# Block-sparse attention before a long-convolution block on one Trainium2 core: mask rows of three head pairs issued from ScalarE's DMA queue, and the last result copied in halves

## The chip, the core and the metric

The kernel runs on one core of one Trainium2 chip. The metric is the device time of the whole program in microseconds (us); lower is better. TensorE (PE in the profile) multiplies matrices, VectorE (DVE), ScalarE (ACT) and GpSimd (POOL) do the rest, SyncE (SP) only issues transfers here. Each engine works through its own instructions in their order, and a semaphore wait holds up all that stands behind it on that engine.

## What is computed

```python
# attention: q, k, v are (4, 8, 768, 64), blocks of 64 positions
k_rep = k.reshape(B, H, 12, 64, D).mean(axis=3)
gate = einsum('bhsd,bhnd->bhsn', q, k_rep)      # future blocks: -1e9
sel = top 3 blocks of gate for each row, and the row's own block
scores = where(sel & causal, q @ k.T / 8, -1e9)
x = softmax(scores) @ v                          # to (4, 768, 512)
# long convolution and gates
x1, x2, x3 = split(x @ w_proj, 3)                # w_proj (512, 1536)
conv = irfft(rfft(x2, axis=1) * rfft(filter_fft, axis=0), axis=1)
out = (x1 * conv * x3) @ w_out                   # float32 (4, 768, 512)
```

## The kernel before

The 32 heads are handled as 16 pairs (p = 0 to 15, four to a batch element). Each head of a pair takes three slots, so a pair has six and the program 96. In a slot n, PE makes the scores of slot n+1 (`scores`, L562, into one of two PSUM buffers, tag "sc", L138), ACT takes the exponential of slot n (L571), POOL zeroes the upper triangles (L574), and PE multiplies the exponentials of slot n-1 with the values (`products`, L596). After a head's third slot DVE divides by the sums (L604, L605) and frees the one PSUM accumulator of the products.

The selected blocks enter the scores as extra contraction rows. For head 0 of pair p the moving operand is `TQ[p % 3]` (its tile is named TQL): rows 0 to 63 hold q transposed, and rows 64 to 75 one mask row for each block. For head 1 it is `QB[p % 2]`, built alike. The stationary operands `KA[p % 2]` and `KB[p % 3]` hold k transposed and twelve rows that mark the blocks. What is made for a pair ahead of its slots:

- q: loaded by SP (`load`, L153), turned by PE (L387) and copied by ACT with all 128 rows into TQ (`copy_q`, L459), with a rest by DVE (L464). From pair five on, ACT casts q (`cast_q`, L471), DVE splits it (L476) and a transposing DMA turns it (L482). Then `part_q` (L485, SP) sends rows 64 to 127 of TQ, the second head's q, to QB.
- k: loaded and turned alike, cast by ACT into KH (`cast_k`, L404), block sums by DVE (L407), and sent by `send_k` (L413 to KA, L414 to KB, both SP).
- mask: PE makes the gate (L490, L496), DVE takes the eight largest of each row and compares (L505, L508, L511), PE turns the result (`turn_mask`, L521), and ACT copies it into `M16[p % 2]` (`copy_mask`, L532). Pairs 0 and 1 write TQ and QB directly; from pair 2 on `send_mask` (L540 to TQ, L541 to QB) sends the rows by DMA, 12 rows of 768 halves each. As these land on rows that `part_q` reads, L540 waits for that pair's L485.

In the first batch element the spectrum of the filter is made beside the attention: SP loads it (`load_filter`, L314, L315), PE reverses it (L332), DVE folds it (L333, L334), PE transforms it (L349), and ACT and DVE turn it by twiddle factors (L370, L376). From pair 4 on the convolution of the batch element before runs in the same slots (`hyena`); the last one runs in a tail after the last slot. There `output` multiplies by w_out (L734), copies the PSUM result (L737) and SP sends it (L738). The last of the tail is O5.

The order is written out by hand in the table ORDER. A time is in sevenths of a slot; `placed` (L816) takes "name.p" if there is one and else adds 42 p to "name:" with p modulo 4. `at` puts the piece into its slot, and the main loop (L889) emits the pieces place by place.

```python
def placed(name, p):
    n0 = 2 * NS * p
    own = ORDER.get(f"{name}.{p}")
    return own if own is not None else 7 * n0 + ORDER[f"{name}:{p % DC}"]
```

In the built program the transfers of SP and ACT share eight semaphores, which are handed out in turn; a transfer waits until the one that had its semaphore before has landed.

Of the kernel before, what the change touches and what calls it, by code (L numbers as in the profile page):

```python
# [37 lines left out]
    "td:3": -48, "kr:3": -57, "g:3": -43, "m:3": -43, "mt:3": -32, "mc:3": -29, "md:3": -28,  # L38
    "v:3": -4, "x:3": 55, "f:3": 66, "k0.1": 1, "k1.1": 1, "q0.1": 11, "q1.1": 13, "kc0.1": 2,
    "ks0.1": 3, "qc0.1": 11, "qr0.1": 13, "kc1.1": 7, "ks1.1": 1, "qc1.1": 13, "qr1.1": 14,  # L40
    "kd.1": 13, "qd.1": 17, "kr.1": 13, "g.1": 18, "m.1": 19, "mt.1": 31, "mc.1": 31, "md.1": 84,
    "k0.2": 12, "k1.2": 27, "q0.2": 31, "q1.2": 39, "kc0.2": 28, "ks0.2": 19, "qc0.2": 37,
    "qr0.2": 39, "kc1.2": 30, "ks1.2": 29, "qc1.2": 39, "qr1.2": 45, "kd.2": 34, "qd.2": 42,
    "kr.2": 42, "g.2": 49, "m.2": 50, "mt.2": 59, "mc.2": 59, "md.2": 62, "k0.3": 51, "k1.3": 61,
    "q0.3": 67, "q1.3": 75, "kc0.3": 55, "ks0.3": 63, "qc0.3": 71, "qr0.3": 79, "kc1.3": 67,
    "ks1.3": 63, "qc1.3": 77, "qr1.3": 80, "kd.3": 67, "qd.3": 92, "kr.3": 66, "g.3": 83, "m.3": 87,
    "mt.3": 100, "mc.3": 102, "md.3": 109, "v.1": 13, "v.2": 53, "v.3": 112, "ldv.2": 23,
    "ldk.3": 11, "ldq.3": 40, "ldv.3": 83, "x.0": 65, "x.1": 105, "x.2": 151, "MN": 6, "flip": 4,
    "cos": 10, "wo": 233, "rows0": 5, "rows1": 28, "rows2": 59, "M0": 43, "M1": 42, "lf0": 18,
    "IC0": 44, "IS0": 32, "ff0": 80, "s00": 109, "s10": 123, "tA00": 128, "tA10": 144, "tB00": 132,  # L50
    "tB10": 136, "t200": 148, "t210": 157, "lf1": 18, "IC1": 42, "IS1": 58, "ff1": 95, "s01": 137,
    "s11": 143, "tA01": 162, "tA11": 168, "tB01": 163, "tB11": 176, "lf2": 81, "IC2": 35, "IS2": 70,
    "ff2": 102, "s02": 158, "s12": 157, "tA02": 175, "tA12": 186, "tB02": 180, "tB12": 196,
# [2 lines left out]
    "hc:0": -94, "hl:0": -100, "hd:0": -85, "hs:0": -66, "hc:1": -86, "hl:1": -75, "hd:1": -64,  # L56
    "hs:1": -57, "hc:2": -117, "hl:2": -114, "hd:2": -99, "hs:2": -110, "hc:3": -94, "hl:3": -93,
    "hd:3": -76, "hs:3": -74, "mq:0": -31, "mq:1": -29, "mq:2": -30, "mq:3": -27, "mq.1": 31,
    "mq.2": 75, "mq.3": 102, "direct": 2,
    "open": ["id32", "zeros", "lq0", "halves", "angles", "lk0", "lk1", "lv0", "twists", "sp0",  # L60
        "sp1", "own", "sp2", "sr0", "w14", "w2", "biasl", "lq1", "MN0", "period", "sr2", "sr1",
        "biasr", "q0", "sm0", "qc0", "q1", "id16", "sm2", "qc1", "qd", "qr0", "sm1", "w8",
        "qr1", "k0", "k1", "ks0", "se2", "ks1", "kc0", "kc1", "se1", "se0", "w2", "kr", "kd",
        "st1", "st2", "st0", "g", "table", "w13", "lk2", "lv1", "m", "rows", "w1", "mt", "ones",
        "ma", "lq2", "mb", "v", "s", "sel16", "late"],
    "mid": [("P00", 29), ("P11", 35), ("P02", 38), ("P01", 44), ("P12", 48), ("F00", 63),
        ("P10", 67), ("X01", 70), ("F10", 74), ("X02", 74), ("F01", 75), ("X00", 83), ("F11",
        92), ("F02", 94), ("F12", 103), ("X03", 103), ("X11", 112), ("X10", 116), ("I3", 122),
# [23 lines left out]
def kernel(  # L92
# [10 lines left out]
    nc = tc.nc  # L103

    B, H, S, D = q.shape
    P = 128
    SC = S // P
    NB = S // 64
    Dm = H * D
# [31 lines left out]
    def one(name, shape=(P, 512), dtype=FP32):  # L141
        return ps.tile(list(shape), dtype, name=name, tag="one", bufs=3)
# [109 lines left out]
    MN = [const.tile([P, SC, P], fp, name=f"MN{i}") for i in range(2)]  # L252
    V16 = [const.tile([P, SC, 2, 66], fp, name=f"V16_{i}") for i in range(3)]
    KA = [const.tile([P, S], fp, name=f"KA{i}") for i in range(2)]
    KB = [const.tile([P, S], fp, name=f"KB{i}") for i in range(3)]

    TQL = [const.tile([P, 2 * SC - 1, P], fp, name=f"TQL{i}") for i in range(3)]
    TQ = [t[:, 0:SC, :].rearrange("p c s -> p (c s)") for t in TQL]
    QL = [t[:, SC - 1:2 * SC - 1, :].rearrange("p c s -> p (c s)") for t in TQL]
    QB = [const.tile([P, S], fp, name=f"QB{i}") for i in range(2)]  # L260
# [40 lines left out]
    flip = const.tile([P, P], FP32, name="flip")  # L301
# [3 lines left out]
    wo = const.tile([P, DC, Dm], fp, name="wo")  # L305
# [104 lines left out]

    def send_k(p):
        kh = KH[p % 2]
        nc.sync.dma_start(KA[p % 2][0:D, :], kh[0:D, :])  # L413
        nc.sync.dma_start(KB[p % 3][0:D, :], kh[D:P, :])  # L414


    def cast_k16(p):
# [96 lines left out]
    M16 = [const.tile([P, S], fp, name=f"M16_{i}") for i in range(2)]  # L514
# [22 lines left out]
                                scalar2=None, op0=ALU.mult)  # L537

    def send_mask(p):
        nc.sync.dma_start(TQ[p % 3][64:64 + NB, :], M16[p % 2][64:64 + NB, :])  # L540
        nc.sync.dma_start(QB[p % 2][64:64 + NB, :], M16[p % 2][96:96 + NB, :])  # L541

# [92 lines left out]
    def hyena(b, spread):  # L637
# [3 lines left out]
        def other(step):  # L641
            return ("m" if spread else "t") + step in ORDER["swap"]
# [20 lines left out]
        def single(step, name, small_bank):  # L663
            return one(name) if small_bank != other(step) else sc_tile()[:, 0:512]
# [66 lines left out]
        def output(i):  # L731
            op = one("op") if spread else single(f"O{i}", "op", True)
            for cc in range(DC):
                nc.tensor.matmul(op, lhsT=st["yT"][:, cc, P * i:P * (i + 1)], rhs=wo[:, cc, :],  # L734
                                 start=(cc == 0), stop=(cc == DC - 1))
            osb = outp.tile([P, Dm], FP32, name="osb", tag="osb")
            (nc.vector.tensor_copy if other(f"C{i}") else nc.scalar.copy)(osb, op)  # L737
            late.append(lambda: nc.sync.dma_start(out[b, P * i:P * (i + 1), :], osb))  # L738

# [9 lines left out]
        for i in range(SC):  # L749
            steps[f"O{i}"] = lambda i=i: output(i)  # L750
# [16 lines left out]
    def ones_of_values():  # L767
# [7 lines left out]
        "biasl": bias_left, "biasr": bias_right, "own": own_blocks,  # L775
        "MN0": lambda: nc.vector.memset(MN[0], 0.0), "rows": mask_rows, "late": constants_late,
        "ones": ones_of_values, "qd": lambda: part_q(0), "kd": lambda: send_k(0),
        "table": lambda: nc.scalar.preload_act_table_set("natural_log_exp_and_others"),
        "kr": lambda: prep_kr(0), "g": lambda: prep_gate(0), "m": lambda: prep_mask(0),
# [30 lines left out]
    def at(time, f):  # L810
        n, place = divmod(time, 7)
        assert n >= 0
        if n < slots:
            work[n][place].append(f)
# [7 lines left out]
    for p in range(NP):  # L822
# [5 lines left out]
        if p:  # L828
            if p < ORDER["kturned"]:
                for t in range(2):  # L830
                    ev += [(f"k{t}", lambda p=p, t=t: turn_k(p, t)),
                           (f"kc{t}", lambda p=p, t=t: cast_k(p, t)),
                           (f"ks{t}", lambda p=p, t=t: sum_k(p, t))]
            else:
                ev += [("hc", lambda p=p: cast_k16(p)), ("hl", lambda p=p: split_k(p)),
                       ("hd", lambda p=p: send_kh(p)), ("hs", lambda p=p: sum_k16(p))]
            ev += [("kd", lambda p=p: send_k(p))]
            if p < TURNED:
                for t in range(2):
                    ev += [(f"q{t}", lambda p=p, t=t: turn_q(p, t)), (f"qc{t}", lambda p=p, t=t: copy_q(p, t)),  # L840
                           (f"qr{t}", lambda p=p, t=t: rest_q(p, t))]
                ev += [("qd", lambda p=p: part_q(p))]
            else:
                ev += [("tc", lambda p=p: cast_q(p)), ("tr", lambda p=p: split_q(p)),
                       ("ts", lambda p=p: send_q(p)), ("td", lambda p=p: part_q(p))]
            ev += [("kr", lambda p=p: prep_kr(p)), ("g", lambda p=p: prep_gate(p)),
                   ("m", lambda p=p: prep_mask(p)), ("mt", lambda p=p: turn_mask(p)),
                   ("mc", lambda p=p: copy_mask(p)), ("v", lambda p=p: prep_v(p))]
            if p >= DIRECT:
                ev += [("md", lambda p=p: send_mask(p))]  # L850
            else:
                ev += [("mq", lambda p=p: copy_second_mask(p))]
# [29 lines left out]
            at(ORDER[name], f)  # L882
    for b in range(1, B):
        steps = hyena(b - 1, True)
        for name, time in ORDER["last" if b == B - 1 else "mid"]:
            at(7 * per * b + time, steps.pop(name))
        rest = steps

# [17 lines left out]
    tail = hyena(B - 1, False)  # L906
# [37 lines left out]
```

## Time and profile before

| | us |
|---|---|
| median of 3 runs | 252.03 |
| lowest and highest | 251.15, 253.54 |
| the profiled execution | 251.01 |
| its span | 249.3 |
| PE busy | 231.0 |
| DVE busy | 190.6 |
| ACT busy | 166.4 |
| POOL busy | 132.2 |

The span runs from the first to the last instruction of the profiled execution. A row of the timeline gives start, length, engine, line, operation, output and input tiles with shapes, and in brackets how long the engine stood idle before and what released it. "SPq" is SP's queue; a row of it is the issue, not the transfer's way to its landing. A row of the chain of work that ended last gives start, length and what it was. In a group's row "x27 | 12.9, 478" is the count, the busy time in us and the mean of one in ns.

### The profile page before, as it was taken

Reading aid. Unit: us, or ns where it says so; the run is one execution under the profiler, and the core shown is the slowest. Engines: PE = TensorE matmul, PEld = TensorE weight load, DVE = VectorE, ACT = ScalarE, POOL = GpSimd, SP = SyncE. Lnnn points to the kernel's source line nnn. Section 1 sums busy time; section 2 is a strip of 40 time slices with the busy share of each in tenths; the row PEclk is TensorE's granted clock in tenths of the full one; section 3 lists DMA queues with packets and bytes.
Section 4 is the critical chain, followed back from the end, with each engine's and each line's share of the span. In section 5 each row is a group of like instructions: output and inputs, shape, how many; then the busy total and the mean of one; then the engine's idle time right before and its main releaser. Section 6 shows DMA issues by size and latency. Waiting matters only on the chain.

```text
span 249.3 us, 6285 instructions
## 1 busy us (share of the span) xinstructions
PE 231.0 (93%) x2270; PEld 151.0 (61%) x2270; DVE 190.6 (76%) x558; ACT 166.4 (67%) x258; POOL 132.2 (53%) x248
## 2 busy tenths in 40 slices
PE   5888988899699999999999999999999999999993
PEld 4666865577556676666574666666656665544551
DVE  3676767878866998988568988896789777668981
ACT  4747975668798568696986577869856776422352
POOL 7623532635573568874432698754257586005560
PEclk9979999999999999999999999999999999999999
DMA  8998968999999996999999979979973111500015
GB/s 161 201 225 218 246 137 221 214 162 216 177 216 208 173 191 144 193 173 203 273 214 203 194 157 180 168 166 260 213 138 66 37 28 51 213 1 0 0 41 214
DMA packets 110295, 40.47 MB, mean 162 GB/s; under 512 B 100932, under 2 KB 106424, under 8 KB 110264
## 3 DMA queue, kind: packets, MB, share of 16 engines
q1 hardware_dynamic: 108008, 37.97, 76.4%
q0 software_dynamic: 2256, 2.10, 5.7%
q8 instruction: 18, 0.29, 0.5%
q14 instruction: 13, 0.11, 0.2%
HBM read 24.64 MB, written 6.29 MB: 124 GB/s over the span
## 4 chain that ended last, share of the span: by engine, by line
PE 70%; DMA 10%; DVE 7%; SPq 5%; ACT 4%; issue 2%; POOL 0%; ACTq 0%; DVEq 0%; POOLq 0%
PE sps L562 11%; PE op L734 7%; PE x2p L658 7%; PE x3p L722 6%; PE o L596 6%; PE x1p L719 6%; PE xx L671 4%; SPq L153 4%; DMA TQL<-M 3%; PE kt L387 3%; PE ye L699 3%; PE yo L702 3%; DMA q_nat<-in_q_dram 2%; DMA QB<-TQL 2%; DMA fb<-in_moe_filter_fft_dram 2%
## 5 line engine op out<-in xcount | busy, mean ns | idle before, releaser
L571 ACT ACTIVATE ex<-sps 128x896 f16<-128x896 f32 x96 | 87.6, 923 | 5.1 <-PE sps L562 4.8
L574 POOL TENSOR_SCALAR_AFFINE_SELECT ex<-ex 128x256 f16<-128x256 f16 x96 | 41.7, 437 | 77.6 <-ACT ex L571 74.0
L596 PEld LDWEIGHTS <-ex 128*128 128x128 f16 x672 | 32.9, 97 | 9.7 <-DVE xnat L605 1.0
L596 PE MATMUL o<-V,ex 128*128 128x65 f16 x672 | 36.4, 193 | 0.5 <-DVE xnat L605 0.2
L562 PE MATMUL sps<-TQL,KA 76*128 76x512 f16 (+1 forms) x144 | 26.4, 293 | 2.5 <-DMA TQL<-M 1.4
L691 POOL TENSOR_TENSOR yT<-gg,yy 128x384 f16<-128x384 f32 x23 | 22.9, 1015 | 8.0 <-DVE yy L708 3.5
L562 PE MATMUL sps<-QB,KB 76*128 76x512 f16 (+1 forms) x144 | 26.2, 290 | 0.2
L725 ACT CAST x1sb<-x1p 128x384 f16<-128x384 f32 x27 | 12.9, 478 | 19.2 <-PE x1p L719 19.1
L682 POOL TENSOR_TENSOR PQ<-ta 128x512 f16<-128x512 f32 x12 | 15.2, 1270 | 19.0 <-DVE ta L681 18.8
L658 PE MATMUL x2p<-wp,xf 128*128 128x512 f16 x96 | 24.2, 379 | 0.0
L719 PE MATMUL x1p<-xT,wp 128*128 128x384 f16 x108 | 22.0, 325 | 0.4 <-ACT x1sb L725 0.4
L722 PE MATMUL x3p<-xT,wp 128*128 128x384 f16 x108 | 22.0, 326 | 0.4 <-DVE tb L677 0.3
L404 ACT CAST KH<-kt 128x384 f16<-128x384 f32 x30 | 14.4, 482 | 11.6 <-PE kt L387 7.2
L734 PE MATMUL op<-wo,yT 128*128 128x512 f16 x84 | 20.6, 379 | 0.0
L407 DVE TENSOR_REDUCE krs<-kt 128x6 f32<-128x384 f32 x30 | 16.4, 553 | 4.9 <-PE kt L387 4.3
L727 DVE TENSOR_TENSOR gg<-x1sb,x3p 128x384 f32<-128x384 f16 x27 | 14.8, 549 | 5.8 <-PE x3p L722 5.8
L562 PEld LDWEIGHTS <-KA 76*128 76x128 f16 x144 | 12.1, 98 | 11.4 <-issue 2.5
L505 DVE MAX8 m<-g 128x8 f32<-128x12 f32 x160 | 13.9, 162 | 6.4 <-PE g L496 6.4
L605 DVE TENSOR_TENSOR xnat<-o,rc 128x384 f16<-128x384 f32 x32 | 17.8, 558 | 1.1
L722 PEld LDWEIGHTS <-wp 128*128 128x128 f16 x128 | 12.5, 98 | 9.1 <-issue 0.9
L590 PE MATMUL o<-zeros 128*128 128x256 f16 x90 | 14.4, 273 | 3.1 <-DVE xnat L605 3.1
L562 PEld LDWEIGHTS <-KB 76*128 76x128 f16 x144 | 12.5, 97 | 7.8 <-issue 0.2
(171 smaller groups left out, 473.7 us busy)
## 6 DMA issues: line engine op xcount, KB each, us to landing
q_nat<-in_q_dram SPq DMA_DIRECT2D x32, 192.0 KB
k_nat<-in_k_dram SPq DMA_DIRECT2D x32, 192.0 KB
v_nat<-in_v_dram SPq DMA_DIRECT2D x32, 192.0 KB
out_dram<-osb SPq DMA_DIRECT2D x24, 256.0 KB
QB<-TQL SPq DMA_DIRECT2D x16, 96.0 KB
KA<-KH SPq DMA_DIRECT2D x16, 96.0 KB
KB<-KH SPq DMA_DIRECT2D x16, 96.0 KB
wp<-in_moe_w_proj_dram POOLq DMA_DIRECT2D x12, 128.0 KB, 4.5
```

The costliest lines, as they stand in the source:

```text
L407: nc.vector.tensor_reduce(out=state["krs", p][:, 6 * t:6 * t + 6], in_=taken("kt", p, t).rearrange("p (n j) -> p n j", j=64), axis=AX.X, o ...
L562: nc.tensor.matmul(t[:, col:col + q1 - q0], lhsT=kk[0:64 + NB, P * kc:P * (kc + 1)], rhs=qq[0:64 + NB, q0:q1], start=True, stop=True, skip ...
L571: nc.scalar.activation(ex, t[:, 0:W], AF.Exp, bias=0.0, scale=EXPS)
L574: nc.gpsimd.affine_select(out=tri, in_=tri, compare_op=ALU.is_ge, fill=0.0, base=0, pattern=[[0, 2], [1, P]], channel_multiplier=-1)
L596: nc.tensor.matmul(o[:, qc, :], lhsT=ex[:, c0:c0 + P], rhs=V16[p % 3][:, kc, h, 0:65], start=first, stop=False, skip_group_check=True)
L605: nc.vector.tensor_tensor(xn[:, :, D * h:D * (h + 1)], o[:, :, 0:D], rc.to_broadcast([P, SC, D]), op=ALU.mult)
L658: nc.tensor.matmul(pa, lhsT=xf[:, eo, dc, P * i:P * (i + 1)], rhs=wp[:, dc, Dm:2 * Dm], start=(dc == 0), stop=(dc == DC - 1))
L682: (nc.vector if other(f"A{j}") else nc.gpsimd).tensor_sub(PQ[:, 0, j, :], t1, ta)
L691: e.tensor_mul(st["yT"][:, dc, F * hf:F * (hf + 1)], g, yy[:, 1, ::-1] if hf else yy[:, 0, :])
L719: nc.tensor.matmul(x1p, lhsT=wp[:, d2, dsl], rhs=xT[:, d2, hs], start=(d2 == 0), stop=(d2 == DC - 1))
L722: nc.tensor.matmul(x3p, lhsT=wp[:, d2, 2 * Dm + P * dc:2 * Dm + P * (dc + 1)], rhs=xT[:, d2, hs], start=(d2 == 0), stop=(d2 == DC - 1))
L734: nc.tensor.matmul(op, lhsT=st["yT"][:, cc, P * i:P * (i + 1)], rhs=wo[:, cc, :], start=(cc == 0), stop=(cc == DC - 1))
```

## The change

`send_k` and `send_mask` choose their queue by the pair; "mact" is 5 and "kact" is 0, so masks of pairs 2, 3 and 4 go through ACT's queue and all k transfers stay on SP's. Many pieces of pairs 4 to 8 get an entry of their own in ORDER, "md.1", "mq.2" and "mq.3" are left out of the table, and the order of the convolution pieces of the first batch element gets its own list, "first". In the tail the last result is copied in two halves, by DVE and ACT, and each half is sent by its own queue.

```diff
-    "kd.1": 13, ... "mc.1": 31, "md.1": 84,
+    "kd.1": 13, ... "mc.1": 31,
-    "mq.2": 75, "mq.3": 102, "direct": 2,
+    "direct": 2, "ldk.4": 53, "ldk.8": 221, "ldq.4": 45, ... "mt.4": 136, "mc.4": 140, "md.4": 148,
+    ... "x.3": 181, "x.7": 349, "f.3": 192, "f.7": 360, "mact": 5, "kact": 0,
+    "first": [["P00", 29], ["P11", 35], ["P02", 38], ... ["O5", 186], ["O1", 195]],
     def send_k(p):
         kh = KH[p % 2]
-        nc.sync.dma_start(KA[p % 2][0:D, :], kh[0:D, :])
-        nc.sync.dma_start(KB[p % 3][0:D, :], kh[D:P, :])
+        queue = nc.scalar if p < ORDER["kact"] else nc.sync
+        queue.dma_start(KA[p % 2][0:D, :], kh[0:D, :])
+        queue.dma_start(KB[p % 3][0:D, :], kh[D:P, :])
     def send_mask(p):
-        nc.sync.dma_start(TQ[p % 3][64:64 + NB, :], M16[p % 2][64:64 + NB, :])
-        nc.sync.dma_start(QB[p % 2][64:64 + NB, :], M16[p % 2][96:96 + NB, :])
+        queue = nc.scalar if p < ORDER["mact"] else nc.sync
+        queue.dma_start(TQ[p % 3][64:64 + NB, :], M16[p % 2][64:64 + NB, :])
+        queue.dma_start(QB[p % 2][64:64 + NB, :], M16[p % 2][96:96 + NB, :])
...
             osb = outp.tile([P, Dm], FP32, name="osb", tag="osb")
+            if not spread and f"O{i}" == ORDER["tail"][-1]:
+                for cols, copy, queue in ((slice(0, Dm // 2), nc.vector.tensor_copy, nc.sync),
+                                          (slice(Dm // 2, Dm), nc.scalar.copy, nc.scalar)):
+                    copy(osb[:, cols], op[:, cols])
+                    queue.dma_start(out[b, P * i:P * (i + 1), cols], osb[:, cols])
+                return
             (nc.vector.tensor_copy if other(f"C{i}") else nc.scalar.copy)(osb, op)
...
-        for name, time in ORDER["last" if b == B - 1 else "mid"]:
+        for name, time in ORDER["first" if b == 1 else "last" if b == B - 1 else "mid"]:
```

## The prediction, made before the result was known

> **What bounds the kernel now.** I read the first part of the page, then the busy time by stretches, then the chain that ended last in the stretch where TensorE is not full.
>
> ```profile
> span 249.3 us, 6285 instructions
> PE 231.0 (93%) x2270; PEld 151.0 (61%) x2270; DVE 190.6 (76%) x558; ACT 166.4 (67%) x258; POOL 132.2 (53%) x248
> wp<-in_moe_w_proj_dram POOLq DMA_DIRECT2D x12, 128.0 KB, 4.5
> ```
>
> In the stretches the first pair of numbers is the stretch, then its length, then PE's busy time.
>
> ```profile
> 30.00:75.00 45.00, 38.98 (x462) 28.07 (x463) 34.73 (x99) 33.39 (x50) 22.19 (x50) 1.00 1.06 192
> 75.00:128.00 53.00, 52.70 (x540) 34.18 (x537) 43.67 (x135) 40.47 (x62) 31.02 (x54) 1.00 1.02 197
> 140.00:245.00 105.00, 104.16 (x905) 62.40 (x903) 83.61 (x202) 64.40 (x102) 57.13 (x82) 1.00 0.54 112
> ```
>
> TensorE is the bound from 75 us on: 0.30 us idle in 53, 0.84 in 105. Between 30 and 75 us it idles 6.02 us, and all moved transfers lie there (33 to 57 us). A delay or gain of PE left over at 75 us goes into the end undiminished; one that PE's idle time swallows is worth nothing. PE's waits in the stretch (idle time and releaser in brackets):
>
> ```profile
> 33.01 0.55 PE L562 MATMUL sps<-QB,KB 76*128 76x384 f16 x3
> 33.89 0.61 PE L590 MATMUL o<-zeros 128*128 128x256 f16 x4 [0.33 <-DVE xnat L605]
> 35.42 0.54 PE L562 MATMUL sps<-TQL,KA 76*128 76x512 f16 x3 [0.35 <-DMA TQL<-M]
> 43.49 1.10 PE L332 MATMUL rev<-fb,flip 128*128 128x512 f32 x2 [1.06 <-DMA fb<-in_moe_filter_fft_dram]
> 50.13 0.54 PE L562 MATMUL sps<-TQL,KA 76*128 76x512 f16 x3 [1.05 <-DMA TQL<-M]
> 63.54 0.38 PE L596 MATMUL o<-V,ex 128*128 128x65 f16 x7
> 66.67 0.28 PE L590 MATMUL o<-zeros 128*128 128x256 f16 x1 [2.38 <-DVE xnat L605]
> ```
>
> The rows at 35.42 and 50.13 are the first scores of pairs two and three waiting for mask rows. SP's queue, start and length (x2: two transfers):
>
> ```profile
> 27.37 0.50 SPq L485 DMA_DIRECT2D QB<-TQL  x1
> 33.27 0.78 SPq L540 DMA_DIRECT2D TQL<-M  x1
> 34.09 0.71 SPq L541 DMA_DIRECT2D QB<-M  x1
> 34.85 0.53 SPq L413 DMA_DIRECT2D KA<-KH  x1
> 36.06 2.63 SPq L153 DMA_DIRECT2D q_nat<-in_q_dram  x2
> 39.33 0.43 SPq L315 DMA_DIRECT2D fb<-in_moe_filter_fft_dram  x1
> 40.93 0.68 SPq L485 DMA_DIRECT2D QB<-TQL  x1
> 43.52 2.07 SPq L153 DMA_DIRECT2D v_nat<-in_v_dram  x2
> 45.97 0.79 SPq L540 DMA_DIRECT2D TQL<-M  x1
> 56.49 0.80 SPq L540 DMA_DIRECT2D TQL<-M  x1
> ```
>
> SP issues nearly without a gap; what stands behind a transfer is late by its length. The chain gives time from issue to landing:
>
> ```profile
> 39.33 4.02 DMA fb<-in_moe_filter_fft_dram
> 45.92 0.01 SPq L540
> 45.97 4.02 DMA TQL<-M
> ```
>
> ScalarE, start and length:
>
> ```profile
> 30.55 0.70 ACT L532 ACTIVATE M<-mt 44x640 f16<-44x640 f16 x1 [0.50 <-PE mt L521]
> 31.27 0.92 ACT L571 ACTIVATE ex<-sps 128x896 f16<-128x896 f32 x1
> 32.26 0.48 ACT L404 CAST KH<-kt 128x384 f16<-128x384 f32 x1
> 43.67 0.92 ACT L571 ACTIVATE ex<-sps 128x896 f16<-128x896 f32 x1
> 44.48 0.84 ACT L471 ACTIVATE q<-q_nat 128x768 f16<-128x768 f32 x1
> 46.36 0.92 ACT L571 ACTIVATE ex<-sps 128x896 f16<-128x896 f32 x1 [1.05 <-PE sps L562]
> 57.54 0.92 ACT L571 ACTIVATE ex<-sps 128x896 f16<-128x896 f32 x1
> 58.34 0.72 ACT L370 ACTIVATE turn<-hsb,tw 128x512 f32<-128x512 f32 x1
> ```
>
> **What the change moves.** Worked out, each new entry of the table equals 42 times p plus the old entry for p modulo 4, and "first" repeats "mid"; md.1, mq.2 and mq.3 differ, but no piece uses them. So the re-placing moves nothing, and apart from the last result only this changes: six issues (two each for pairs two, three and four, counted from 0) leave SP's queue and stand in ScalarE's, right behind the M copy for pair two, one ex further for pair three, behind the ex at 57.54 for pair four. With them their waits move: the mask rows overwrite rows that the pair's QB<-TQL transfer (L485) reads, so the issue waits until that has landed. On SP that held up loads; on ScalarE it holds up exponentials. I take ScalarE's issue as long as SP's, 0.78 + 0.71 with two gaps of 0.04 (34.09 less 33.27 less 0.78): 1.57 us for two. No ScalarE issue is in the trace; below it is bounded by 0.43 (the fb row), above by half of 2.63. The Trainium skill, Perfetto Trace Analysis (DMA Instruction — HWDGE), says that an issue locks the descriptor generator for itself, and that waiting for the lock is inside the reported length. By that the sum would be rival B's; with only SP issuing, no run here shows it.
>
> **Pair two.** When does its QB<-TQL, issued at 27.37, land? For pair three the same transfer was issued at 40.93; its mask issue had SP free at 43.52 + 2.07 = 45.59, the other things it waits for (fb landed at 39.33 + 4.02 = 43.35, the M copy) were over, and it was released at 45.92. So that took 4.99 us, though the profile names a DVE instruction. By this row 27.37 + 4.99 = 32.36; by the 4.02 of the others 31.39; later than 33.27 is excluded, as SP had passed the wait then. I take 32.36, the same transfer under the same load. ScalarE is done with M at 31.25, waits 1.1 us, issues 1.57, and starts ex at 33.93 instead of 31.27: 2.66 late. This ex frees one of two score buffers: the scores at 33.01 start at 33.93 + 0.92 = 34.87 with the gap, 1.86 late. PE's idle 0.33 and 0.35 behind it cover 0.68; the scores at 35.42 are 1.18 late. The mask itself left 0.9 us earlier and is no longer last.
>
> The KH cast at 32.26 moves to 34.92 and ends at 35.40. SP's L413 waits for it, so SP, now 1.58 us lighter (34.85 less 33.27), goes on at 35.44, not earlier but 0.59 later than 34.85; the saving is spent waiting. fb is issued at 39.92, lands at 43.94, and PE's rev starts 0.59 late. PE, 1.18 late, reaches it at 43.61 and loses no more: its 1.06 of idle time covers the rest. PE stands at +0.59. Bounds: with 4.02 in place of 4.99 all of this shifts 0.97 down, to PE at about -0.38 behind rev.
>
> **Pair three.** Its QB<-TQL goes out at 41.52 and lands at 46.51. ScalarE comes to the issue at 45.8 at the latest (43.67 + 1.18 + 0.92), waits, issues until 48.08, then q (44.48 before), then ex at 48.08 + 0.84 = 48.92 instead of 46.36, done at 49.84. Queued behind the wait are q, whose split DVE makes, and two exponentials. The mask leaves at 46.51, 0.54 later than before, since the same landing released it on SP; with the 4.02 of the same tile it lands at 50.53 and the scores at 50.13 go at 50.67. The ex is done 0.8 us before that. PE is at +0.54. Bounds: the mask can land in 2.15 us, as it did for pair two (33.27 to the scores at 35.42); then the ex, at 49.86, is last, and PE is at -0.27.
>
> **Pair four.** Its QB<-TQL landed long before; only the issue counts. Behind it stand turn, the next q and the exponentials of two groups. ScalarE, +0.54, issues at 58.88 and does turn at 60.45 instead of 58.34, done at 61.17. DVE wants it:
>
> ```profile
> 60.51 0.75 DVE L376 SCALAR_TENSOR_TENSOR A<-hsa,tw,turn 128x512 f16<-128x512 f32 x1
> 65.49 0.72 ACT L370 ACTIVATE turn<-hsa,tw 128x512 f32<-128x512 f32 x1 [0.25 <-DVE Asb L376]
> 66.06 0.56 DVE L605 TENSOR_TENSOR xnat<-o,rc 128x384 f16<-128x384 f32 x1
> ```
>
> A, due at 61.05, starts at 61.19: DVE is at +0.68, and with it xnat, which ends PE's 2.38. The mask leaves 2.4 us later than at 56.49 and lands near 62.9, 1.2 late for the first scores of pair four; the products at 63.54 then end by 65.2, before xnat asks for them at 66.06. If DVE's backlog were not there, this 1.2 and ScalarE's 2.1 would show. ScalarE has its idle time back before pair five's mask, which SP still sends. PE is at +0.68 at 75 us.
>
> **The last result.** Its copy before, and the copies that give its price by width:
>
> ```profile
> 245.38 0.59 ACT L737 COPY osb<-op 128x512 f32<-128x512 f32 x1 [1.18 <-PE op L734]
> L725 ACT CAST x1sb<-x1p 128x384 f16<-128x384 f32 x27 | 12.9, 478 | 19.2 <-PE x1p L719 19.1
> 34.55 0.42 DVE L464 SCALAR_TENSOR_TENSOR TQL<-qt,TQL 128x256 f16<-128x256 f32 x1
> ```
>
> ScalarE's half by the slope: 0.59 less 2 x 0.112 = 0.37; DVE's at most 0.42. The later half is ready 0.17 to 0.22 sooner: -0.20. The bytes stay the same; with an issue of 0.78 on ScalarE in place of 0.43 it would be +0.15, and I keep -0.25 to +0.15.
>
> **Sum.** +0.68 - 0.20 = +0.48. The profiled execution took 251.01 us (span 249.3), so 251.5; it stands 1.02 under the median of the runs, 252.03, so the forecast is 252.5 for the median. With pair two's lower bound it is -0.38 + 0.14 - 0.20, 251.6. With ScalarE's issues at 1.0 us each, 0.5 more per pair, pair three's scores go at 51.17 and pair four adds 0.64: +1.5, 253.5.
>
> **Rivals.** A, faster: ScalarE's queue carries nothing else, so masks land in 2.15 us instead of 4.02, and QB<-TQL lands in 4.02. Then SP is 0.38 early, pair three's QB<-TQL lands at 44.57 and PE reaches 50.13 less 1.05 less 0.38 = 48.70 without a wait: -1.43, +0.14 from DVE, -0.20: 250.5. Only if the 0.35, 1.06 and 1.05 all vanish is it -2.66, 249.4. For it: pair two's 2.15. Against: POOL's queue, also one of its own, needed 4.5 us (the wp row). The Trainium skill, DMA: Bandwidth & Descriptors (Queues, rings and completion order), has each DMA engine take turns between queues by packets; that would be A, and the 4.5 us does not bear it out.
>
> B, slower: ScalarE's issue cannot run beside SP's and waits for the one in progress. SP's are 1.0 to 1.3 us in the rows x2, so each of six issues grows by up to 1.0. Pair two's two add 2.0 to ex and to the KH cast, hence to SP and to pair three's QB<-TQL; pair three adds 2.0 more, and the ex there, 49.84 + 4.0, is last: +3.7; pair four's 2.0 mostly fall under PE's 2.38: about +4, 256.0. It decides from about 0.5 a piece: ex at 51.84, +1.7, pair four +1.0, the copy -0.2, together +2.5. SP's nearly gapless queue speaks for it; against it that SP itself stands waiting at 35 us.
>
> C, nothing: the waits on ScalarE fall into idle time and only the last copy counts: 251.8.
>
> **Chances.** Forecast 0.50 (its own range 251.6 to 253.6), A 0.17, B 0.20, C 0.13. Of A 0.06 loses all three waits and is faster by over 1%; B is slower by over 1%; the rest, 0.74, is within 1%, about what a measurement of this kernel can tell from no change. The range 250.4 to 254.9 leaves out that 0.06 and 0.13 of B.
>
> **What would show it.** Right: ex behind pair two's M starts near 33.9 with the gap put down to ScalarE's queue; SP's L413 near 35.4; rev near 44.1 with less idle before it; scores of pair three near 50.7; xnat's wait near 67.3. Wrong: ex within 1.6 us of M, issues over 1.2 us on ScalarE, or pair three's scores before 49.8.

## The result and the profile after

| | before | changed |
|---|---|---|
| median, us (runs) | 252.00 (4) | 255.79 (4) |
| lowest, highest | 251.15, 253.54 | 254.48, 256.38 |
| the profiled execution, its span | 251.01, 249.3 | 255.38, 253.5 |

The ratio of the changed kernel to the kernel before is 1.0128 (95% interval 1.0084 to 1.0171): 1.3% slower, where 252.5 us was forecast. Two later comparisons of the same kernel gave 1.0050 (0.9999 to 1.0100) and 1.0084 (1.0042 to 1.0126), so the change costs between 0.5 and 1.3%, and part of the first gap is the spread between comparisons. Ratios leave out runs of over 1.5% above the fastest of the same kernel, so they can differ from the quotient of two medians.

The page's first lines, then the stretches (the column before the last two is the granted clock of TensorE). Behind the change, lines are 22 to 31 higher: L562 is now L586, L605 L629, L540 L564, L571 L595, L413 L436.

```profile
span 253.5 us, 6292 instructions
PE 232.4 (92%) x2270; PEld 151.6 (60%) x2270; DVE 191.5 (76%) x559; ACT 166.1 (66%) x258; POOL 131.9 (52%) x248
...
30.00:75.00 45.00, 37.70 (x429) 27.16 (x427) 34.45 (x98) 30.42 (x45) 20.25 (x46) 0.96 1.00 178
50.00:55.00 5.00, 3.28 (x38) 1.99 (x35) 2.72 (x5) 2.23 (x4) 2.37 (x6) 0.69 0.98 155
75.00:128.00 53.00, 51.05 (x520) 33.04 (x519) 42.45 (x122) 39.26 (x61) 32.15 (x58) 1.00 1.06 187
```

PE does 1.28 us less between 30 and 75 us than before (38.98), 1.65 less between 75 and 128 (52.70), and between 50 and 55 us it has a lower clock, which before it had nowhere in this stretch. PE's rows with its waits:

```profile
36.18 0.54 PE L586 MATMUL sps<-QB,KB 76*128 76x384 f16 x3 [2.60 <-ACT ex L595]
37.57 0.55 PE L586 MATMUL sps<-TQL,KA 76*128 76x512 f16 x3
44.62 1.13 PE L354 MATMUL rev<-fb,flip 128*128 128x512 f32 x2
51.95 0.91 PE L586 MATMUL sps<-TQL,KA 76*128 76x512 f16 x3 [1.72 <-DMA k_nat<-in_k_dram]
54.86 0.73 PE L586 MATMUL sps<-TQL,KA 76*128 76x512 f16 x3
69.81 0.28 PE L614 MATMUL o<-zeros 128*128 128x256 f16 x1 [2.10 <-DVE xnat L629]
76.31 0.56 PE L586 MATMUL sps<-TQL,KA 76*128 76x512 f16 x3 [0.47 <-DMA TQL<-M]
91.61 0.54 PE L586 MATMUL sps<-TQL,KA 76*128 76x512 f16 x3 [1.17 <-DMA TQL<-M]
```

Against the rows of before: 36.18 was 33.01 (3.17 late), 37.57 was 35.42 (2.15 late), 44.62 was 43.49 (1.13), 51.95 was 50.13 (1.82) and 69.81 was 66.67 (3.14). The second scores of pair three stand at 54.86, 2.91 us behind the first; before it was 1.67. ScalarE, then SyncE:

```profile
30.80 0.70 ACT L555 ACTIVATE M<-mt 44x640 f16<-44x640 f16 x1 [0.50 <-PE mt L544]
33.07 1.33 ACTq L564 DMA_DIRECT2D TQL<-M  x1
34.44 0.73 ACTq L565 DMA_DIRECT2D QB<-M  x1
35.21 0.92 ACT L595 ACTIVATE ex<-sps 128x896 f16<-128x896 f32 x1 [3.71 <-DMA TQL<-M]
45.82 0.92 ACT L595 ACTIVATE ex<-sps 128x896 f16<-128x896 f32 x1
46.88 0.78 ACTq L564 DMA_DIRECT2D TQL<-M  x1
48.48 0.84 ACT L494 ACTIVATE q<-q_nat 128x768 f16<-128x768 f32 x1 [1.75 <-DMA k_nat<-in_k_dram]
60.47 0.74 ACTq L564 DMA_DIRECT2D TQL<-M  x1
62.03 0.72 ACT L392 ACTIVATE turn<-hsb,tw 128x512 f32<-128x512 f32 x1 [0.32 <-issue]
```

```profile
32.68 0.79 SPq L833 DMA_DIRECT2D KB<-KA  x1
36.53 0.48 SPq L436 DMA_DIRECT2D KA<-KH  x1
46.44 1.60 SPq L175 DMA_DIRECT2D k_nat<-in_k_dram  x2
```

ScalarE stands idle for 3.71 us between M and ex, and SyncE, which the change was to relieve, for 3.06 us (33.47 to 36.53), because KH is cast behind that ex. Of the 3.71 us, 1.57 are the wait (from M's end at 31.50 to 33.07) and 2.14 the two issues and their gaps. At pair three there is no such wait: ScalarE ends ex at 46.74 and issues at 46.88, and nearly all of its 1.75 us idle is the two issues. Two landings from the chain of work:

```profile
27.33 5.56 DMA QB<-TQL
...
84.77 6.80 DMA TQL<-M
```

### The profile page after: what moved, and what is told of

Same layout as the page of the kernel before. It is cut to its first block, busy times and chain, and to the rows that moved or that the text cites. A ratio compares the mean times of both kernels' runs of the same rounds, so it can differ in the third digit from the quotient of the medians.

```text
span 253.5 us, 6292 instructions
## 1 busy us (share of the span) xinstructions
PE 232.4 (92%) x2270; PEld 151.6 (60%) x2270; DVE 191.5 (76%) x559; ACT 166.1 (66%) x258; POOL 131.9 (52%) x248
## 4 chain that ended last, share of the span: by engine, by line
PE 57%; DMA 17%; DVE 9%; ACT 7%; POOL 3%; issue 3%; SPq 2%; ACTq 1%; POOLq 0%; DVEq 0%
PE sps L586 9%; PE op L758 7%; PE x2p L682 7%; PE o L620 5%; DMA TQL<-M 5%; PE x1p L743 4%; PE x3p L746 4%; DMA QB<-TQL 4%; ACT ex L595 4%; DMA q_nat<-in_q_dram 3%; DMA v_nat<-in_v_dram 3%; PE xx L695 3%; PE ye L723 2%; PE yo L726 2%; PE kt L409 2%
## 5 line engine op out<-in xcount | busy, mean ns | idle before, releaser
L595 ACT ACTIVATE ex<-sps 128x896 f16<-128x896 f32 x96 | 87.6, 923 | 7.9 <-PE sps L586 4.0
L586 PE MATMUL sps<-TQL,KA 76*128 76x512 f16 (+1 forms) x144 | 27.3, 301 | 5.0 <-DMA k_nat<-in_k_dram 1.7
L586 PE MATMUL sps<-QB,KB 76*128 76x512 f16 (+1 forms) x144 | 26.2, 289 | 2.8 <-ACT ex L595 2.6
L586 PEld LDWEIGHTS <-KA 76*128 76x128 f16 x144 | 12.5, 99 | 14.5 <-issue 4.4
L586 PEld LDWEIGHTS <-KB 76*128 76x128 f16 x144 | 12.5, 97 | 10.5 <-issue 3.0
L629 DVE TENSOR_TENSOR xnat<-o,rc 128x384 f16<-128x384 f32 x32 | 17.8, 558 | 1.1
## 6 DMA issues: line engine op xcount, KB each, us to landing
out_dram<-osb SPq DMA_DIRECT2D x23, 256.0 KB, 3.6
```

What stands on the lines that cost most here:

```text
L586: nc.tensor.matmul(t[:, col:col + q1 - q0], lhsT=kk[0:64 + NB, P * kc:P * (kc + 1)], rhs=qq[0:64 + NB, q0:q1], start=True, stop=True, skip ...
L595: nc.scalar.activation(ex, t[:, 0:W], AF.Exp, bias=0.0, scale=EXPS)
L629: nc.vector.tensor_tensor(xn[:, :, D * h:D * (h + 1)], o[:, :, 0:D], rc.to_broadcast([P, SC, D]), op=ALU.mult)
```

## The experiments

The first theory, H: ScalarE's queue is held while the mask pieces wait for QB<-TQL to land, and everything behind them, exponentials first, is held with it. Rivals: I, each issue on ScalarE costs its own length wherever it stands; C, TensorE's clock drops behind a long wait, and this makes more of the delay.

**One pair at a time.** The first kernel has no mask on ScalarE's queue (only the last result's halves remain), the others one pair each.

```diff
-        queue = nc.scalar if p < ORDER["mact"] else nc.sync
+        queue = nc.scalar if p in () else nc.sync
```

> All masks back on SP, only the last result in halves. If the loss comes from ScalarE's six issues (every theory but one), this is 252.0 within 0.7, since in the changed kernel the end of the last product to the end of the span is 3.97 us against 3.99 before. If the halves cost by themselves, it is nearer 255.8 than 252.

The next three have `p in (2,)`, `p in (3,)` and `p in (4,)` in that line.

```diff
+        queue = nc.scalar if p in (2,) else nc.sync
```

> Only pair two's masks on ScalarE, halves as in the changed kernel. Theory H (ScalarE's queue is held by the wait for the landing of QB<-TQL, 1.6 us, and SP and pair three follow late): most of the 3.8 us, 254.5 to 256. Rival I (each issue on ScalarE costs its length, alike for all pairs): a third, 253.3. Rival C (PE's clock drops after a long idle time ahead of pair three's scores, which only the sum of pairs two and three reaches): under 253.

```diff
+        queue = nc.scalar if p in (3,) else nc.sync
```

> Only pair three's masks on ScalarE. H: the mask is released by the same landing as before, near 45.9, so it leaves no later; ScalarE holds q and one ex until 47.5, and this ex ends near 49.2, before the scores at 50.1: 252.0 to 252.6. I: 253.3. C: under 253.

```diff
+        queue = nc.scalar if p in (4,) else nc.sync
```

> Only pair four's masks on ScalarE. H: no landing to wait for, and in the changed kernel ScalarE stood only 0.3 us for these two issues: 251.5 to 252.4. I: 253.3.

Measured: none 1.0025 (0.9981 to 1.0070), pair two 1.0062 (1.0014 to 1.0110), pair three 1.0043 (0.9995 to 1.0090), pair four 1.0017 (0.9967 to 1.0066). Only pair two's interval leaves out 1. For pair four no cost shows. The medians are 253.38, 253.79 and 251.75 us for pairs two, three and four: H's ranges missed the first two and took in the third, and I's 253.3 fits the first and misses the last. So these times alone do not decide between H and I.

**Two pairs, and the whole change again.**

```diff
+        queue = nc.scalar if p in (2, 3) else nc.sync
```

> Only the masks of pairs two and three go by ScalarE's queue. If the delays of the pairs simply add up: pair two alone was 0.37% and pair three alone 0.18% above the kernel with no mask on ScalarE's queue, which was itself 0.25% above the kernel before, so ratio 1.0080, about 253.5 us. Theory C (the clock that TensorE is granted drops for about 3.4 us after a stretch in which it idled; only the two pairs together bring the stall that triggers it near 52 us): more than the sum, a ratio near that of the whole change, 1.0128, with a granted clock near 0.7 in the window from 50 to 55 us.

The second is the changed kernel, unaltered.

> The whole change once more, unaltered, beside the others of this call. If the whole change costs what its first comparison showed: ratio 1.0128, between 1.008 and 1.017. If a part of that was the chip and not the change: near the sum of the pairs' own costs, 1.0072.

Measured: 1.0120 (1.0073 to 1.0168) and 1.0050 (0.9999 to 1.0100). Two of the pairs came out above all three, so the intervals, about 0.5% to either side, are the limit here: whether the pairs add up or make more together is not settled by these times.

**Work for TensorE in the gap at 52 us.** The 14 more matmuls add zeros.

```diff
-     4, 20: 2, 21: 4, 12: 1, 30: 4, 26: 2, 13: 4, 28: 2, 7: 5, 11: 1, 15: 4, 8: 1, 5: 2, 33:
+     4, 20: 2, 21: 4, 12: 1, 30: 4, 26: 2, 13: 4, 28: 2, 7: 5, 11: 1, 15: 18, 8: 1, 5: 2, 33:
```

> The whole change, with 14 more matmuls of the zeros tile ahead of scores(18), about 1.5 us of TensorE's work at the place where it waits 1.72 us for the mask of pair three; their product is added as zeros, as before. Theory C: TensorE is no longer idle there, the granted clock from 50 to 55 us stays at 1.00 instead of 0.69, and the run is about 1.2 us shorter than the whole change (ratio 1.008). Rival: the low clock is by chance or follows from something else; then the 14 matmuls bring nothing, or cost up to 1.5 us where the mask would have been there in time (ratio 1.013 to 1.019).

Measured: 1.0073 (1.0032 to 1.0114), beside 1.0050 for the whole change in the same comparison: no gain. Its stretches:

```profile
35.00:40.00 5.00, 3.23 (x20) 2.29 (x20) 0.95 (x3) 2.85 (x5) 1.45 (x5) 0.60 0.31 70
40.00:45.00 5.00, 5.00 (x51) 3.28 (x49) 3.00 (x14) 1.86 (x4) 0.82 (x2) 0.72 1.08 271
50.00:55.00 5.00, 4.58 (x47) 3.35 (x45) 4.74 (x10) 3.09 (x5) 3.75 (x9) 1.00 0.69 116
```

The low clock isn't at 50 us but at 37, behind pair two's wait, which this edit left in place. The whole change beside it has its low clock there too (0.66 from 35 to 40). So the fill was at the wrong one of two gaps in this execution, and says nothing on the price.

**Pair two's pieces nine places later.** They then stand behind ex(10), when QB<-TQL has landed. The first of these kernels has only pair two's masks on ScalarE's queue.

```diff
-    "g.2": 49, "m.2": 50, "mt.2": 59, "mc.2": 59, "md.2": 62, "k0.3": 51, "k1.3": 61, "q0.3": 67,
+    "g.2": 49, "m.2": 50, "mt.2": 59, "mc.2": 59, "md.2": 71, "k0.3": 51, "k1.3": 61, "q0.3": 67,
-        queue = nc.scalar if p < ORDER["mact"] else nc.sync
+        queue = nc.scalar if p in (2,) else nc.sync
```

> Only the mask of pair two goes by ScalarE's queue, and its two pieces are issued nine places later in ScalarE's order, behind ex(10) and not ahead of it. Theory H (ScalarE's queue is held while the pieces wait for QB<-TQL to land, and all that ScalarE has behind them is held too): ScalarE's idle 3.7 to 4.3 us ahead of ex goes, TensorE's wait of 2.73 us for ex at 36.3 us goes or turns into a wait of under 1.5 us for the mask itself, and SyncE's KA<-KH is issued before 36.0 us instead of at 36.6. Theory I (each issue costs its own length wherever it stands): same as with pair two in its own place, TensorE's wait stays at 2.7 us within 0.3.

Its one run took 252.03 us. In it TensorE's wait for ex is gone and SyncE's KA<-KH goes out at 34.73, as H has it. The same kernel was then measured in ten runs, and so was, twice, the kernel without the second edit, that is with pairs three and four on ScalarE's queue as in the change:

> Only the mask of pair two goes by ScalarE's queue, behind ex(10); the masks of pairs three and four go by SyncE's queue as in the kernel before. If the gain of the mended version comes from the part of pair two (1.5 us of issues are taken from SyncE there, and nothing waits for them): 0.995 to 0.999. If it comes from pairs three and four: 1.000 to 1.004.

> The whole change with pair two's two pieces issued behind ex(10), as in the look at pair two alone: ScalarE's idle 3.7 us near 35 us and TensorE's wait of 2.6 us there go. If the cost of the change is mostly that: 1.1 us less than the whole change, so a ratio of 1.001 to 1.004 (the whole change gave 1.0128 and 1.005 beside the kernel before). If the pairs behind it cost what is saved: 1.005 or more.

> The mended version once more: the whole change with the two pieces of pair two issued behind ex(10). If its gain in the first comparison was the placement: ratio 0.993 to 0.999, and below the whole change by 0.8% or more. If it was that chip or chance: 1.000 to 1.004.

> The whole change, unaltered, beside its mended version on one chip. Its two comparisons gave 1.0128 and 1.005. If the placement of the pieces of pair two is the cause of the loss: 1.005 to 1.013 here, and the mended version 0.8% or more under it.

The last is the changed kernel, unaltered, beside the one with pair two late. Measured: late pair two alone 0.9929 (0.9887 to 0.9971); the whole change with pair two late 0.9952 (0.9908 to 0.9995) and 0.9940 (0.9900 to 0.9981); beside the latter the whole change as it was, 1.0084 (1.0042 to 1.0126). The first two came out faster than expected. Nine places make 1.44%, 3.6 us, and the two intervals are apart. ScalarE, SyncE and PE of the kernel with late pair two alone:

```profile
31.48 0.70 ACT L555 ACTIVATE M<-mt 44x640 f16<-44x640 f16 x1 [0.50 <-PE mt L544]
32.20 0.92 ACT L595 ACTIVATE ex<-sps 128x896 f16<-128x896 f32 x1
33.19 0.48 ACT L426 CAST KH<-kt 128x384 f16<-128x384 f32 x1
33.36 1.59 ACTq L564 DMA_DIRECT2D TQL<-M  x1
33.57 0.92 ACT L595 ACTIVATE ex<-sps 128x896 f16<-128x896 f32 x1
35.82 0.87 ACT L482 ACTIVATE TQL<-qt 128x384 f16<-128x384 f32 x2 [1.33 <-DMA k_nat<-in_k_dram]
```

```profile
33.70 0.48 SPq L436 DMA_DIRECT2D KA<-KH  x1
38.30 1.50 SPq L337 DMA_DIRECT2D fb<-in_moe_filter_fft_dram  x1
```

```profile
36.10 0.54 PE L586 MATMUL sps<-TQL,KA 76*128 76x512 f16 x3
43.14 1.13 PE L354 MATMUL rev<-fb,flip 128*128 128x512 f32 x2
```

ScalarE does ex and the KH cast right behind M, and the issue, though at 1.59 us the longest of these, runs while ex works at 33.57. SyncE sends KA<-KH as soon as KH is cast. The two waits of before, 0.35 for the mask and 1.06 for fb, are gone. So an issue does not cost its length wherever it stands, which was I, and pair two's early place is what the change loses by. H is right about the wait but is not the whole of it: behind ex(10) the lengths of the issues, too, are partly covered by work that ScalarE has in progress. What is left is 1.33 us idle ahead of 35.82, and TensorE does not wait for what comes behind it (before, ScalarE stood idle for 1.17 there).

**Pairs three and four alone.**

```diff
+        queue = nc.scalar if p in (3, 4) else nc.sync
```

> Only the masks of pairs three and four go by ScalarE's queue. By the cost of each pair alone, 0.18% for pair three and 0.08% less than nothing for pair four, over the kernel with none, which stood 0.25% over the kernel before: 1.0035. If pair two in its place was the whole loss, and the rest gains: below 1.000.

Measured: 1.0022 (0.9974 to 1.0069); the interval takes in no change. The whole change beside it had 1.0084, but the two intervals overlap.

**The queue or the place?** All masks on SyncE's queue, and pair two's nine places later all the same; then late pair two with pair four.

```diff
+    "g.2": 49, "m.2": 50, "mt.2": 59, "mc.2": 59, "md.2": 71, "k0.3": 51, "k1.3": 61, "q0.3": 67,
+        queue = nc.scalar if p in () else nc.sync
```

> All masks on SyncE's queue; only, the two pieces of pair two stand nine places later, which puts them behind the transfers KA<-KH and KB<-KH of SyncE's order and not ahead of them. If the later place alone makes the gain of 0.7% that pair two showed when it went late on ScalarE's queue: 0.992 to 0.996. If SyncE must be rid of the two issues for it (filter and k loads behind them then come 1.5 us sooner): 0.999 to 1.004.

```diff
+    "g.2": 49, "m.2": 50, "mt.2": 59, "mc.2": 59, "md.2": 71, "k0.3": 51, "k1.3": 61, "q0.3": 67,
+        queue = nc.scalar if p in (2, 4) else nc.sync
```

> The masks of pair two, late, and of pair four on ScalarE's queue, that of pair three on SyncE's. Pair two late alone gave 0.9929, with pairs three and four behind it 0.9940 and 0.9952; pair three alone cost 0.18% and pair four nothing. If these add up: 0.992 to 0.995.

Measured: late on SyncE's queue 1.0013 (0.9975 to 1.0050); pairs two, late, and four on ScalarE's 0.9897 (0.9849 to 0.9945), median 249.25 us beside 252.16, a little below what was expected. The later place alone brings nothing. There the mask has to go behind KA<-KH and KB<-KH and PE waits for it:

```profile
34.66 0.78 SPq L564 DMA_DIRECT2D TQL<-M  x1
```

```profile
37.29 0.54 PE L586 MATMUL sps<-TQL,KA 76*128 76x512 f16 x3 [1.87 <-DMA TQL<-M]
```

With two queues, mask and k go out side by side. Pairs two, late, and four make the lowest ratio measured here, from six runs; its interval overlaps that of late pair two alone.

**Why pair three's mask lands late.** The two k_nat loads at 46.4 us are put behind the transposing transfer; in the run they go out at 56.64.

```diff
-    "ldk.6": 112
+    "ldk.6": 125
```

> The whole change, but the two k_nat loads that SyncE issues at about 46.5 us, right as the mask of pair three goes out on ScalarE's queue, go out after the transposing transfer, some 6 us later. In the whole change and its parts this mask needed 5.0 to 5.5 us from its issue to the first scores. If the loads in flight slow it (in the kernel before they stood behind the mask in SyncE's own order): 4.1 us or less, TensorE's wait for it under 0.9 us. If ScalarE's queue is slow to start its packets whatever else moves: 4.8 us or more, the wait as before.

One run, 254.35 us. ScalarE and PE:

```profile
48.28 0.77 ACTq L564 DMA_DIRECT2D TQL<-M  x1
```

```profile
52.52 0.55 PE L586 MATMUL sps<-TQL,KA 76*128 76x512 f16 x3
```

PE waits for no mask; it was there 4.24 us behind its issue at the latest, against 5.07 in the change. So in this pair of executions the loads beside it account for at least 0.8 us, and a queue that is slow by itself is not borne out. The other profiles agree: with the loads beside it on ScalarE's queue the mask of pair three took 5.0 to 5.5 us from issue to scores in eight profiles, and 4.0 to 4.9 in the seven that wait for it on SyncE's queue, ahead of the loads.

**Each half in its own tile.** All masks on SyncE's queue.

```diff
+                osb2 = outp.tile([P, Dm], FP32, name="osb", tag="osb")
+                for cols, t, copy, queue in ((slice(0, Dm // 2), osb, nc.vector.tensor_copy, nc.sync),
+                                             (slice(Dm // 2, Dm), osb2, nc.scalar.copy, nc.scalar)):
+                    copy(t[:, cols], op[:, cols])
```

> All masks on SyncE's queue, and the two halves of the last result in a tile each. If ScalarE's half waited for VectorE's only because both write one tile: the two copies start within 0.1 us of each other, and from the end of the last product to the end of the span it is 3.6 to 3.7 us in place of 3.97. If something else keeps them apart (both read one PSUM bank): as before, 3.9 to 4.0.

One run, 251.97 us. The copies (the changed kernel has them alike, at 249.61 and 250.07):

```profile
246.36 0.42 DVE L765 COPY osb<-op 128x256 f32<-128x256 f32 x1 [0.23 <-PE op L758]
...
246.86 0.37 ACT L765 COPY osb<-op 128x256 f32<-128x256 f32 x1 [1.70 <-DVE osb L765]
```

ScalarE's half still starts when VectorE's has ended. In the built program its copy still waits for VectorE; the tile that both halves still share is `op`, which both read.

**The other big wait, shortened.** The kernel before, with xnat ahead of two of VectorE's pieces.

```diff
-    "tA11": 168
+    "tA11": 173, "ks0.6": 173
```

> The kernel before without the change; only, VectorE divides the result of the head that ends near 64 us ahead of two pieces that it does first otherwise (Asb, 0.66 us, and krs, 0.46 us). TensorE's wait for xnat at 66.7 us, 2.38 us, should fall to about 1.3. If the time is set by TensorE's idle stretches before 75 us and by nothing later: 1.1 us less, ratio 0.9955, and a little better than that if stretches of about 2 us are what brings the low granted clock behind them (seen near 66 to 72 us in several of the other kernels). If it is given back later (masks of pairs five and six that TensorE then reaches too early): ratio 0.998 to 1.001.

Measured: 1.0008 (0.9978 to 1.0039). The wait fell, and the next one came:

```profile
65.92 0.28 PE L590 MATMUL o<-zeros 128*128 128x256 f16 x1 [1.25 <-DVE xnat L605]
69.93 0.54 PE L562 MATMUL sps<-QB,KB 76*128 76x512 f16 x3 [1.65 <-ACT ex L571]
```

```profile
67.50 0.72 ACT L370 ACTIVATE turn<-hsa,tw 128x512 f32<-128x512 f32 x1 [1.88 <-DVE Asb L376]
```

ScalarE's turn needs Asb, one of the pieces put back, and ex stands behind turn. In this profile the 1.13 us were given back 4 us later.

## Why the prediction was wrong

What failed is the sum of delays. At the matmul behind xnat's wait TensorE was forecast 0.68 us late and was 3.14 late. Three steps make the difference: pair three's mask was issued 0.37 later than forecast, as pair two's terms were too small, its landing took 0.9 longer, and a slower clock, which the sum put at nothing, took 1.24. A wait of 1.17 us at 91.61, which was not forecast either, brings the end to 4.22.

One table shows it by the profiles. Executions differ already at 30 us, where M, the mask rows of pair two, is made, so places are given from M's start: first the first scores of pair three, then the matmul behind xnat's wait (66.67 before). It has the kernels on which the reading rests. The clock column names the 5 us stretch in which the granted clock first falls.

| masks on ScalarE's queue | scores | behind xnat | granted clock below 1 between 30 and 60 us | ratio |
|---|---|---|---|---|
| before | 19.58 | 36.12 | no | 1 |
| none, with halves | 19.10 | 35.66 | no | 1.0025 |
| none, pair two late on SyncE's | 18.94 | 35.48 | no | 1.0013 |
| three | 19.55 | 37.60 | at 50 | 1.0043 |
| four | 19.41 | 36.43 | no | 1.0017 |
| three, four | 19.84 | 37.79 | at 50 | 1.0022 |
| two | 21.49 | 38.05 | at 35 | 1.0062 |
| two, three | 21.28 | 39.33 | at 50 | 1.0120 |
| whole change (its three profiles) | 21.15, 22.32, 20.94 | 39.01, 38.76, 37.38 | at 50, at 35, at 30 | 1.0128, 1.0050, 1.0084 |
| whole, pair two late | 19.26, 18.58 | 35.69, 35.02 | no | 0.9952, 0.9940 |
| two late (its two profiles) | 18.30, 18.06 | 34.85, 34.58 | no | 0.9929 |
| two late, four | 17.71 | 34.00 | no | 0.9897 |

**Pair two: the mechanism was right, the size was not.** ScalarE waits for QB<-TQL, ex is late, PE waits for ex, SyncE's L413 comes later and not earlier: all as said. Two terms were too small. The landing of QB<-TQL took 5.56 us, not 4.99, and came at 32.89 instead of 32.36, with the issue beginning 0.18 behind it; and the first issue took 1.33 us, not 0.78, and stands just above the bound that the prediction gave for an issue, half of 2.63. So ex started at 35.21 where 33.93 was forecast: 0.53 + 0.18 + 0.57 = 1.28 more. SyncE's KA<-KH followed at 36.53, not 35.44, and PE's first mask-bound scores of the pair stood 2.15 us late, not 1.18. fb's idle 1.06 covered what it was said to cover: rev was 1.13 late, not 0.59.

**Pair three: the landing.** The issue at 46.88 came 0.37 behind the forecast 46.51, but not for the reason given: ScalarE did not wait for QB<-TQL. It was at ex until 46.74, as PE was 2.15 us late and not 1.18, and found the landing over. The scores came 5.07 us behind the issue, where the forecast had 4.16 (4.02 and a gap of 0.14). The 4.02 was taken from a mask that on SyncE's queue stood ahead of the k_nat loads; moving it off that queue let those loads (46.44) go out beside it. The step "with the 4.02 of the same tile" left out what SyncE would now send sooner. The wait is put down to a k_nat load in the row; the scores use the mask, and the kernel with the loads moved shows no wait.

**The clock: not in the prediction at all.** From the first to the second scores of pair three it took 2.91 us instead of 1.67: 1.24 us, with a granted clock of 0.69 from 50 to 55. Lines of the changed kernel and of the kernel before, in stretches of the length for which the clock is low:

```profile
48.44:51.85 3.41, 1.38 (x16) 0.85 (x13) 2.18 (x7) 2.83 (x4) 1.71 (x4) 1.00 1.04 208
51.85:55.26 3.41, 3.31 (x31) 1.91 (x32) 1.63 (x5) 0.92 (x1) 1.23 (x4) 0.50 1.19 139
...
62.59:66.01 3.42, 1.70 (x20) 1.28 (x18) 3.35 (x8) 3.17 (x6) 2.22 (x6) 1.00 1.25 187
66.01:69.42 3.41, 2.60 (x37) 2.21 (x38) 2.68 (x6) 2.11 (x4) 1.19 (x3) 1.00 1.25 165
```

The clock is at half, 0.50, for 3.41 us. In the 20 profiles it is below 1 between 30 and 60 us in nine, and all nine have the mask of pair two or three in its early place on ScalarE's queue. Of the eleven others only the two of the whole change with pair two late have such a mask, pair three's, and TensorE waited only 0.99 and 0.79 us for it. In eight of the nine the low stretch lies behind a wait of pair two (2.7 us) or three (1.7 to 2.3); in one, the third of the whole change, behind a wait of 1.87 for KB<-KA ahead of both, so that one is not the change's doing. Pair three alone has the scores at 19.55, as before, and xnat 1.48 late.

Not every such wait brings it: pair two's of 2.60 here and xnat's of 2.38 before did not. The traces show why. In each, the low stretches lie on a grid of 3.41 us, and what counts is TensorE's idle time within one step of that grid. Between 20 and 245 us, in all 20 profiles, twenty steps at full clock had 1.77 to 2.61 us idle, and each was followed by a step at half clock; of the others, up to 1.74 us, none was. Here the step from 48.44 had 2.03 us idle. Pair two's wait of 2.60 fell on two steps, with 1.21 and 1.39, and before the change the step from 62.59 had 1.72. Ahead of 20 us steps with as little as 1.20 us idle were followed by a low one too, so this is not the whole rule. The Trainium skill, TensorE: Matmul & The Clock Gate (What's actually happening), has the clock judged over a window of about 3.4 us that runs free of the program, and the traces agree, with 3.41 us; its rule of thumb (Why this matters for your kernels), no idle gaps above about 3 us, is too lenient here, where the low clock followed a wait of 1.72 us. How much of the change's 0.5 to 1.3% is the clock's is not separated by the times.

**Pair four: overpriced.** Its landing was over, and ScalarE lost 0.32 us and not 1.57. The issues, 60.47 to 61.98, ran while the exponential that stands before them was still to be worked (60.79 to 61.71); ScalarE's queue goes ahead of its arithmetic.

**The last result: nothing, where -0.20 was said.** The halves run one behind the other. From PE's last product to the end it is 3.97 us, before 3.99.

**What is left at 75 us.** "A delay left over at 75 us goes into the end undiminished" held roughly for delays (3.14 late at xnat; the last group of products, 246.76 against 242.54, is 4.22 late, after a wait of 1.17 at 91.61 for pair six's mask, which took 6.80 to land). That wait wasn't foreseen, and isn't explained: the other two profiles of this kernel don't have it. For a gain it is not to be trusted: the kernel with xnat earlier lost its 1.13 us at once, while the kernels with late pair two, 0.4 to 2.1 us earlier at xnat, kept theirs.

**The rivals.** B forecast 256.0, close to the measured 255.79, but by luck. Its mechanism, an issue that waits for SyncE's, isn't there: ScalarE's issue at 46.88 stands in the middle of SyncE's two from 46.44 to 48.04 and takes 0.78, and the one at 60.47 takes 0.74. The Trainium skill, Perfetto Trace Analysis (DMA Instruction — HWDGE), has each issue lock the descriptor generator; these rows do not show the second queue waiting for it. Each program's first mask issue on ScalarE takes 1.33 to 1.59 us, wherever it stands. With pair four alone it begins at 56.53, with no issue of SyncE's in progress, and takes 1.34, so this is not B's wait either. Where it stands late, TensorE does not wait for it. A was right that SyncE's relief is worth something, but pair two's wait took it away; with that mended it is 0.5 to 1.0%. The masks do not land faster, though: pair three's took 5.0 to 5.5 us on ScalarE's queue and 4.0 to 4.9 on SyncE's. The Trainium skill, DMA: Bandwidth & Descriptors (Rules for kernel authors), says that spreading transfers over issuing engines brings no bandwidth and only saves issue time; late pair two on ScalarE's queue against late on SyncE's, 0.9929 and 1.0013, is in line with that, as the mask is issued 1.88 us behind M's start instead of 3.75.

## What to carry to other kernels

A transfer that must wait belongs on a queue whose engine has nothing else due; put on a computing engine's queue, it goes behind the work that would otherwise stand waiting, at a place where the wait is already over. Price a moved transfer by what the queue it leaves will now send sooner, and take landings from rows under the load that will then be there. A wait of about 2 us on TensorE may cost another microsecond behind it in clock (1.24 us here), so the row behind a wait is read together with the granted clock.

## What the hardware showed unasked

- TensorE's granted clock falls to half for 3.41 us when about 1.75 us or more of the 3.41 us step before it were idle (twenty steps of 1.77 us or more, none of 1.74 or less, from 20 us on). So a wait of 1.7 to 2.7 us brings it in some executions and not in others, by where it falls on the grid.
- The first mask issue on ScalarE's queue takes 1.33 to 1.59 us, later ones 0.73 to 0.79. Why is open.
- ScalarE issues a transfer while its arithmetic still works on the instruction before; what stands behind the issue waits for its end (0.32 us idle at pair four, 1.75 at pair three, where nothing was in progress).
- Two copies of one PSUM tile by two engines ran one behind the other because the program has one wait for the other. Whether they could run side by side was not tried.
